# One-hot clusters kept twice, 32 rows apart, in a routed attention and bilinear FFN kernel

## The chip, the cores and the metric

The kernel runs on one core of a Trainium2 chip. A core has five engines that run side by side, each with its own instruction stream: TensorE (PE, with its weight loader PEld), VectorE (DVE), ScalarE (ACT), GpSimd (POOL) and SyncE (SP), which here only issues DMAs. The metric is the device time of one execution in microseconds (us), the median over several executions. The profile is of one execution; its "span" runs from the first to the last instruction.

## The reference

Attention in which a query sees only the keys of its own cluster, for 4 batches, 8 heads, 768 positions, head size 64, with 16 clusters; then a feed-forward block with a bilinear gate on 3072 tokens.

```python
q_assign = np.argmax(np.einsum('bhsd,hcd->bhsc', q_n, c_n), axis=-1)   # q_n, k_n, c_n: normalized
k_assign = np.argmax(np.einsum('bhsd,hcd->bhsc', k_n, c_n), axis=-1)
mask = q_assign[:, :, :, None] == k_assign[:, :, None, :]
scores = scale * np.matmul(q, k.transpose(0, 1, 3, 2))
scores = np.where(mask, scores, -1000000000.0)
...                                             # softmax over keys
attn_out = np.matmul(attn, v)
x = attn_out.transpose(0, 2, 1, 3).reshape(B * S, H * D)
return (x @ w_a) * (x @ w_b) @ w_out            # 512 -> 1536 -> 512
```

## The kernel before

**Pairs and groups.** Heads go two at a time: 16 pairs (4 batches of 4 pairs), `p` in the code. Head a = 0 lies on partitions 0 to 63, head a = 1 on 64 to 127. A pair's scores are made transposed, keys on the PSUM partitions: a unit `u` is one block of 128 keys (`j`, 0 to 5) against one half of the queries (`hf`, 384 of them), for both heads. Two units make a group, so a pair has 6 groups and the kernel 96. The main loop (L987) runs over groups `g`. In each, TensorE gets the scores of this group (`score`, L500), the product with v of the group before (`weigh`, L543), steps that prepare the next pair, and then pieces of the feed-forward block of an earlier batch, by a credit counter, until the next group.

**The mask as a matmul.** The cluster of every query and key is held as a one-hot vector of 16 rows per head, in bf16, in the tile `ohT`. For a key the row of its cluster holds 0 and the others a very large negative number; for a query the row of its cluster holds 1. The product of the two over those rows is 0 where the clusters agree and very negative where they don't. `score` writes it into PSUM first (L508, `start=True`), and the float32 product of q and k adds to it (L517, `stop=True`). ScalarE then takes the exponential (L524). A mask matmul multiplies over all 64 rows of its head, though only 16 carry clusters: the rest of the query rows hold zeros, left there by the first pairs, which write all 128 rows.

**Order inside `score`.** All four mask matmuls of a group stand first: unit 0 head 0, unit 0 head 1, unit 1 head 0, unit 1 head 1. Then the four score products in the same order, each of which the profile shows as two matmuls (float32 goes in two passes). Each of the four has its own PSUM bank. [...] In the profile the form "64*128" is a matmul over 64 rows with 128 output columns, "128*128" one over all rows, "128*64" and "128*32" ones with 64 and 32 output columns.

**How the one-hots come about.** For pairs 0 to 3 TensorE transposes them (`prep_onehot`, L394). For pairs 4 to 15 (`by_blocks`, L186, true from p = 4) VectorE transposes 32x32 blocks (`prep_by_blocks`, L411). That leaves four quarters `kq` of 384 positions each on partitions 32 kq: quarters 0 and 1 are the queries' halves, 2 and 3 the keys'. Within a quarter head a is on 16 rows. `one_hot_across` (L443) then moves each quarter of each head to its place in `ohTs[p]` with a small DMA on SP's queue: 4 quarters by 2 heads, 8 copies of 16 rows by 384 bf16, 12 KB each (L448). This is step 4 of the next pair's six, so it is issued during the fifth group of a pair, and the next pair's first group reads it. `ohTs` has two buffers.

**SP's queue.** One queue, in program order: the loads of q and k (L198), v (L235), weights (L263, two raw buffers), the one-hot copies (L448) and the output stores (L622). Each DMA signals on one of a few semaphores in turn.

Of the kernel before, what the change touches and what calls it, by code (L numbers as in the profile page):

```python
# [136 lines left out]
def short_path(nc, tc, ctx, c, cn, centroids_in, casts, n_far, q, k, v,  # L137
# [3 lines left out]
    B, H, S, D = q.shape  # L141
    NC = 16
# [6 lines left out]
    HB = S // 2  # L149
# [36 lines left out]
    def by_blocks(p):  # L186
        return p >= HP
# [141 lines left out]
    qkTs, ohTs, sims = {}, {}, {}  # L329
# [81 lines left out]
    def prep_by_blocks(p):  # L411

        qkTs[p] = qtp.tile([P, 2 * S], FP32, name="qkT")
        ohTs[p] = ohT_bufs[p % 2]
        NG = 24
        QT = slice(0, P // 2)
        KT = slice(P // 2, P)
        shape = (P, NG, NC)
        sim = simp.tile([P, NG, NC], FP32, name="sim")
        mx = small.tile([P, NG], FP32, name="mx")  # L420
        first = small.tile([P, NG], FP32, name="first")
        oh = oh_all[:, 0:3].rearrange("p n (g c) -> p (n g) c", c=NC)
        ohT = oh_all[:, 3:6].rearrange("p n e -> p (n e)")
        top = lambda t: t[:, :, None].broadcast_to(shape)
        v = nc.vector

        def across(w):
            v.transpose(out=qkTs[p][:, w * S:(w + 1) * S],
                        in_=qks[p][:, w].rearrange("p j d -> p (j d)"))

        def sims_across():
            v.transpose(out=sim.rearrange("p g c -> p (g c)"),
                        in_=sims[p][:, 0:HB])

        def one_hot():


            nc.gpsimd.tensor_tensor(out=oh[KT], in0=sim[KT], in1=top(first)[KT],
                                    op=ALU.subtract)
            v.tensor_tensor(out=oh[QT], in0=sim[QT], in1=top(first)[QT],  # L440
                            op=ALU.is_equal)

        def one_hot_across():  # L443
            v.transpose(out=ohT, in_=oh.rearrange("p g c -> p (g c)"))
            for a in range(2):
                for kq in range(4):
                    r = 32 * kq + a * NC
                    nc.sync.dma_start(  # L448
                        out=ohTs[p][a * D:a * D + NC, kq * HB:(kq + 1) * HB],
                        in_=ohT[r:r + NC, :])  # L450

        return [
            [lambda: across(0), lambda: across(1)],
            [sims_across],
            [lambda: v.tensor_reduce(out=mx, in_=sim, axis=AX.X, op=ALU.max),
             lambda: v.tensor_tensor(out=sim, in0=sim, in1=top(mx), op=ALU.is_ge),
             lambda: v.tensor_tensor(
                 out=sim, in0=sim, in1=rank_far[:, None, :].broadcast_to(shape),
                 op=ALU.mult),
             lambda: v.tensor_reduce(out=first, in_=sim, axis=AX.X, op=ALU.max)],  # L460
            [one_hot],
            [one_hot_across],
            [],
        ]
# [30 lines left out]
    def where(u):  # L495
        p, l = divmod(u, UPP)
        hf, j = divmod(l, NJ)
        return p, hf, j

    def score(us):  # L500
        tiles = []
        for u in us:
            p, hf, j = where(u)
            s = ps_s.tile([P, 2, 512], FP32, name="s")
            tiles.append(s)
            for a in range(2):
                r = slice(a * D, (a + 1) * D)
                nc.tensor.matmul(  # L508
                    out=s[:, a, 0:HB],
                    lhsT=ohTs[p][r, S + j * P:S + (j + 1) * P],  # L510
                    rhs=ohTs[p][r, hf * HB:(hf + 1) * HB],
                    start=True, stop=False)
        for u, s in zip(us, tiles):
            p, hf, j = where(u)
            for a in range(2):
                r = slice(a * D, (a + 1) * D)
                nc.tensor.matmul(  # L517
                    out=s[:, a, 0:HB],
                    lhsT=qkTs[p][r, S + j * P:S + (j + 1) * P],
                    rhs=qkTs[p][r, hf * HB:(hf + 1) * HB],  # L520
                    start=False, stop=True)
        for u, s in zip(us, tiles):
            pt = ptp.tile([P, 2, HB], FP32, name="pt")
            nc.scalar.activation(out=pt, in_=s[:, :, 0:HB], func=AF.Exp,  # L524
                                 scale=SCALE)
            probs[u] = pt
# [460 lines left out]
    for g in range(NG + 3):  # L987
        p, l = divmod(g, GPP)
# [4 lines left out]
        if g < NG:  # L993
            score(now)
# [300 lines left out]
```

## Time and profile before

| | us |
|---|---|
| median of 3 executions | 1072.19 (1072.11 to 1074.16) |
| the profiled execution | 1073.11, span 1071.4 |
| TensorE busy | 1046.6 |
| VectorE busy | 713.7 |
| GpSimd busy | 355.8 |
| ScalarE busy | 259.0 |

The granted TensorE clock is 0.995 of full. "Busy" is the union of an engine's instructions, and the end of a matmul is modelled by the profiler: two matmuls of one form overlap in the records, and a short gap between them need not show as idle. The starts are recorded, so the distance between two starts tells what the array really did. In the page's groups the score products (L517) hold 140.7 us of TensorE's busy time and those with v (L549) 145.1 us; the mask matmuls' group (L508) holds 48.2 us for 384 of them in 96 groups.

### The profile page before, as it was taken

Reading aid. Unit: us, or ns where it says so; the run is one execution under the profiler, and the core shown is the slowest. Engines: PE = TensorE matmul, PEld = TensorE weight load, DVE = VectorE, ACT = ScalarE, POOL = GpSimd, SP = SyncE. Lnnn points to the kernel's source line nnn. Section 1 sums busy time; section 2 is a strip of 40 time slices with the busy share of each in tenths; the row PEclk is TensorE's granted clock in tenths of the full one; section 3 lists DMA queues with packets and bytes.
Section 4 is the critical chain, followed back from the end, with each engine's and each line's share of the span. In section 5 each row is a group of like instructions: output and inputs, shape, how many; then the busy total and the mean of one; then the engine's idle time right before and its main releaser. Section 6 shows DMA issues by size and latency. Waiting matters only on the chain.

```text
span 1071.4 us, 13000 instructions
## 1 busy us (share of the span) xinstructions
PE 1046.6 (98%) x4719; PEld 602.5 (56%) x4719; DVE 713.7 (67%) x1396; ACT 259.0 (24%) x500; POOL 355.8 (33%) x329
## 2 busy tenths in 40 slices
PE   5999999999999999999999999999999999999997
PEld 3444455454556665454545766455455687555686
DVE  5888978787857537766666746667665745676762
ACT  4565423333322221122121221221212200000000
POOL 1221244454542323434444522344344410222200
PEclk8999999999999999999999999999999999999999
DMA  4335352525120120202030030300000000000001
GB/s 140 91 83 91 90 123 82 123 83 136 66 49 15 31 53 14 45 4 45 2 45 2 24 65 13 56 1 19 1 4 1 6 30 25 0 1 1 0 30 33
DMA packets 120504, 46.18 MB, mean 43 GB/s; under 512 B 106608, under 2 KB 115824, under 8 KB 120432
## 3 DMA queue, kind: packets, MB, share of 16 engines
q1 hardware_dynamic: 119456, 43.40, 17.9%
q10 hardware_dynamic: 976, 1.87, 0.5%
q8 instruction: 39, 0.64, 0.3%
q14 instruction: 33, 0.27, 0.1%
HBM read 37.78 MB, written 6.29 MB: 41 GB/s over the span
## 4 chain that ended last, share of the span: by engine, by line
PE 93%; DVE 5%; issue 0%; DMA 0%; POOL 0%; ACT 0%; DVEq 0%; POOLq 0%
PE m L732 30%; PE m L851 19%; PE O L549 12%; PE m L632 12%; PE s L517 11%; PE s L508 4%; PE m L572 3%; PE m L353 1%; DVE raw L693 1%; PE m L337 1%; DVE raw L715 1%; DVE xT L693 0%; DVE acc L538 0%; PE m L399 0%; DVE size L693 0%
## 5 line engine op out<-in xcount | busy, mean ns | idle before, releaser
L524 ACT ACTIVATE pt<-s 128x768 f32<-128x768 f32 x192 | 145.3, 809 | 313.7 <-PE s L517 258.5
L538 POOL TENSOR_TENSOR acc<-acc,pt 128x384 f32<-128x384 f32 x144 | 151.9, 1068 | 59.8 <-ACT pt L524 43.5
L747 POOL TENSOR_TENSOR h<-h,ha 128x384 f32<-128x384 f32 x72 | 72.6, 1016 | 235.8 <-DVE ha L742 234.3
L549 PE MATMUL O<-pt,v 128*64 128x384 f32 x768 | 145.1, 499 | 0.0
L517 PE MATMUL s<-qkT 64*128 64x384 f32 x768 | 140.7, 486 | 0.0
L742 DVE TENSOR_TENSOR ha<-ha,m 128x384 f32<-128x384 f32 x126 | 66.8, 546 | 74.1 <-PE m L732 73.3
L742 DVE TENSOR_TENSOR h<-h,m 128x384 f32<-128x384 f32 x126 | 67.4, 549 | 68.5 <-PE m L732 67.7
L538 DVE TENSOR_TENSOR acc<-acc,pt 128x384 f32<-128x384 f32 x96 | 72.8, 787 | 35.4 <-POOL acc L538 35.0
L549 PEld LDWEIGHTS O<-pt,v 128*64 128x64 f32 x768 | 46.6, 136 | 86.4 <-issue 82.1
L604 POOL TENSOR_TENSOR xT<-xT,acc 128x384 f32<-128x384 f32 x32 | 33.3, 1039 | 169.7 <-DVE acc L599 139.2
L517 PEld LDWEIGHTS s<-qkT 64*128 64x128 f32 x768 | 71.1, 188 | 32.0 <-issue 0.6
L851 PE MATMUL m<-wo_sb,h 128*128 128x256 f32 x384 | 87.5, 382 | 0.0
L851 PEld LDWEIGHTS m<-wo_sb,h 128*128 128x128 f32 x384 | 72.1, 190 | 16.0 <-issue 4.2
L732 PE MATMUL m<-raw 128*128 128x384 f32 x192 | 70.2, 488 | 0.9 <-DVE ha L742 0.9
L632 PE MATMUL m<-xT,wa_sb 128*128 128x384 f32 x192 | 67.1, 492 | 0.0
L632 PE MATMUL m<-xT,wb_sb 128*128 128x384 f32 x192 | 66.8, 491 | 0.0
L851 PE MATMUL m<-xT,h 128*128 128x256 f32 x288 | 65.4, 382 | 0.1
L851 PEld LDWEIGHTS m<-xT,h 128*128 128x128 f32 x288 | 54.1, 190 | 11.7 <-issue 1.7
L732 PE MATMUL m<-xT,wa_sb 128*128 128x384 f32 x144 | 53.0, 491 | 0.0
L732 PE MATMUL m<-xT,size 128*128 128x384 f32 x144 | 52.9, 490 | 0.0
L732 PE MATMUL m<-xT,wb_sb 128*128 128x384 f32 x144 | 52.9, 490 | 0.0
L632 PEld LDWEIGHTS m<-xT,wa_sb 128*128 128x128 f32 x192 | 35.5, 190 | 29.4 <-issue 3.6
(159 smaller groups left out, 1446.4 us busy)
## 6 DMA issues: line engine op xcount, KB each, us to landing
raw<-in_moe_w_out_dram SPq DMA_DIRECT2D x12, 512.0 KB, 3.4
raw<-in_moe_w_a_dram SPq DMA_DIRECT2D x11, 512.0 KB, 3.8
raw<-in_moe_w_b_dram SPq DMA_DIRECT2D x11, 512.0 KB, 3.6
qk<-in_q_dram SPq DMA_DIRECT2D x48, 96.0 KB, 3.1
qk<-in_k_dram SPq DMA_DIRECT2D x48, 96.0 KB, 3.6
v<-in_v_dram SPq DMA_DIRECT2D x24, 192.0 KB, 3.9
out_dram<-rest SPq DMA_DIRECT2D x24, 128.0 KB, 1.7
ohT<-oh SPq DMA_DIRECT2D x96, 12.0 KB, 1.8
```

The lines of the kernel that those rows point to most:

```text
L508: nc.tensor.matmul(out=s[:, a, 0:HB], lhsT=ohTs[p][r, S + j * P:S + (j + 1) * P], rhs=ohTs[p][r, hf * HB:(hf + 1) * HB], start=True, stop= ...
L517: nc.tensor.matmul(out=s[:, a, 0:HB], lhsT=qkTs[p][r, S + j * P:S + (j + 1) * P], rhs=qkTs[p][r, hf * HB:(hf + 1) * HB], start=False, stop ...
L524: nc.scalar.activation(out=pt, in_=s[:, :, 0:HB], func=AF.Exp, scale=SCALE)
L538: eng.tensor_tensor(out=acc[:, a, :], in0=probs[u - 1][:, a, :] if j == 1 else acc[:, a, :], in1=probs[u][:, a, :], op=ALU.add)
L549: nc.tensor.matmul(out=O_of[0][a * D:(a + 1) * D, 0:HB], lhsT=vs[p][:, a, j, :], rhs=probs[u][:, a, :], start=(j == 0), stop=(j == NJ - 1))
L572: nc.tensor.matmul(out=ps[a * D:(a + 1) * D, 0:HB], lhsT=ones, rhs=t[:, a, :], start=(n == 0), stop=(n == len(terms) - 1))
L604: nc.gpsimd.tensor_tensor(out=x, in0=x, in1=den, op=ALU.mult)
L632: nc.tensor.matmul(out=ps[:, 0:HB], lhsT=w_sb[:, ch, f * P:(f + 1) * P], rhs=xTs[b][:, ch, t0:t0 + HB], start=(ch == 0), stop=(ch == NCH - 1))
L732: nc.tensor.matmul(out=ps[:, 0:HB], lhsT=A[l][c], rhs=rhs[c], start=(c == 0), stop=(c == 1))
L742: nc.vector.tensor_tensor(out=out, in0=in0, in1=ps, op=op)
L747: nc.gpsimd.tensor_tensor(out=to, in0=to, in1=box[name], op=ALU.mult)
L851: nc.tensor.matmul(out=ps[:, 0:HN], lhsT=A[l][f // 3][:, f % 3, :], rhs=B[r][f // 2][:, f % 2, :], start=(f == 0), stop=(f == N2 - 1))
```

## The change

For pairs 4 to 15 every one-hot is kept twice: on rows 0 to 15 of its head's 64, as before, and again on rows 32 to 47. The mask matmuls of the second unit of a group read the second copy. Each mask matmul of these pairs now multiplies over 32 rows (16 of clusters and 16 that give zero) instead of 64, so the four of a group lie on rows 0 to 31, 64 to 95, 32 to 63 and 96 to 127. The number of DMAs of `one_hot_across` goes from 8 to 16 a pair, and their order changes: keys' first half, queries' first half, queries' second half, keys' second half, both heads and both copies of each before the next. The score products, and all of pairs 0 to 3, stay as they were. No instruction of VectorE, ScalarE or GpSimd changes.

```diff
         def one_hot_across():
             v.transpose(out=ohT, in_=oh.rearrange("p g c -> p (g c)"))
-            for a in range(2):
-                for kq in range(4):
+
+            for kq in (2, 0, 1, 3):
+                for a in range(2):
                     r = 32 * kq + a * NC
-                    nc.sync.dma_start(
-                        out=ohTs[p][a * D:a * D + NC, kq * HB:(kq + 1) * HB],
-                        in_=ohT[r:r + NC, :])
+                    for n in range(2):
+                        r0 = a * D + 32 * n
+                        nc.sync.dma_start(
+                            out=ohTs[p][r0:r0 + NC, kq * HB:(kq + 1) * HB],
+                            in_=ohT[r:r + NC, :])
...
     def score(us):
         tiles = []
-        for u in us:
+        for n, u in enumerate(us):
             p, hf, j = where(u)
             s = ps_s.tile([P, 2, 512], FP32, name="s")
             tiles.append(s)
             for a in range(2):
                 r = slice(a * D, (a + 1) * D)
+                if by_blocks(p):
+                    r = slice(a * D + 32 * n, a * D + 32 * n + 32)
                 nc.tensor.matmul(
                     out=s[:, a, 0:HB],
```

## The prediction

> **What bounds the kernel now.** I read the page first: the share of busy time, then the chain that ended last, by engine.
>
> ```profile
> PE 1046.6 (98%) x4719; PEld 602.5 (56%) x4719; DVE 713.7 (67%) x1396; ACT 259.0 (24%) x500; POOL 355.8 (33%) x329
> ...
> PE 93%; DVE 5%; issue 0%; DMA 0%; POOL 0%; ACT 0%; DVEq 0%; POOLq 0%
> ```
>
> TensorE is busy all the time and the chain runs through it, so a nanosecond saved or added in TensorE's stream is one in the span. The list of TensorE's waits on other engines holds under 19 us, most of it in the first 20 us. What the page hides is that "busy" includes the gaps between matmuls, since their ends are modelled. So I read the mask matmuls' own line next.
>
> ```profile
> L508 PEld LDWEIGHTS <-ohT x384: 92/95/110, 17.1 to 853.7; 64*128 64x128 bf16 x192
> L508 PE MATMUL s<-ohT x384: 322/332/524, 17.4 to 853.9; 64*128 64x384 bf16 x192
> ...
>   issue: 43.3, 90
> ```
>
> Before 90 of the 96 mask groups the weight loader stands idle for nothing that the profile can name, 0.48 us each. To see why, I took the timeline in narrow windows around one group of pair 12, first the matmuls into and through the group (columns: start, us from start to last end, engine, line, operation; the last number counts matmuls).
>
> ```profile
> 606.92 0.59 PE L851 MATMUL m<-wo_sb,h 128*128 128x256 f32 x2
> ...
> 607.35 0.38 PE L851 MATMUL m<-wo_sb,h 128*128 128x256 f32 x1
> 607.66 0.50 PE L508 MATMUL s<-ohT 64*128 64x384 bf16 x4
> 607.84 0.33 PE L508 MATMUL s<-ohT 64*128 64x384 bf16 x2
> 608.00 0.48 PE L517 MATMUL s<-qkT 64*128 64x384 f32 x1
> 608.97 0.49 PE L517 MATMUL s<-qkT 64*128 64x384 f32 x2
> 609.38 0.54 PE L549 MATMUL O<-pt,v 128*64 128x384 f32 x2
> 609.75 0.49 PE L549 MATMUL O<-pt,v 128*64 128x384 f32 x2
> ```
>
> Starts, not durations, are to be read. Two L851 matmuls of one kind start 0.22 apart (606.92 to 607.35 is two steps), which is their streaming time. From the last of them (128 rows, 128 columns of the array) to the first mask matmul (64 rows) it is 0.31: 0.09 more. The masks run two at a time, second pair 0.17 to 0.18 after the first, and the score products follow 0.16 later: no extra, because both are "64*128". Score pairs follow each other by 0.32 (two passes of 384 float32 columns). From the last to L549, of form "128*64", it is 0.41: again 0.09 more. The loads and the way out of two more forms:
>
> ```profile
> 607.84 0.19 PEld L517 LDWEIGHTS s<-qkT 64*128 64x128 f32 x1
> 610.82 0.30 PEld L851 LDWEIGHTS m<-wo_sb,h 128*128 128x128 f32 x2 [0.60 <-issue]
> 611.14 0.19 PEld L851 LDWEIGHTS m<-wo_sb,h 128*128 128x128 f32 x1
> 622.32 0.49 PE L353 MATMUL m<-qkT,cTb 128*32 128x384 f32 x1
> 622.74 0.54 PE L572 MATMUL m<-acc,ones 128*64 128x384 f32 x2
> ```
>
> The score weights are loaded while the second mask pair runs (607.84), so nothing shows. After a change of form they aren't: L851's first load stands at 610.82 beside its first matmul, the next matmul comes at 611.14, 0.32 later where 0.22 is its rate. Even 128*32 to 128*64, one column tiling to another, costs 0.42 for a 0.32 stream. Every change of form in this trace costs **0.09 to 0.10 us of emptying, and then the first weight load in the open**: 0.10 for 128 float32 columns (L851), 0.05 for 64 (L549: 0.37 against 0.32), 0.01 for 128 bf16 columns (the mask pair's 0.17 against 0.16).
>
> [...] The trace shows two row groups at once (mask pairs) and four column groups (L353), no four row groups. [...]
>
> **The change, part by part.** It touches pairs 4 to 15, 12 pairs of 6 groups: 72 groups; the other 24 keep 64-row masks.
>
> 1. Four masks at once. Before: 607.66 to 608.00, 0.335 us from first mask to first score (0.173 + 0.162 by the medians of the starts). After: four starts 3 ns apart (0.01), the first load 0.01, one stream 0.16, so 0.18 if nothing else came: 0.154 saved.
> 2. A new change of form, 32-row masks to 64-row scores. The way into the masks is a change already, and the way out of the scores too; this one is added. [...] Bounds: nothing, or what the five kinds of change seen cost, 0.09 to 0.10. I take 0.095, as none was free, columns to columns included.
> 3. The score weights' load comes into the open: 128 float32 columns, 0.10 (L851; 0.104 in the unrounded starts). Bounds 0 (loaded while the masks run, as now) and 0.10; I take 0.10, as no load went ahead of a change of form.
>
> Sum per group: −0.154 + 0.095 + 0.104 = +0.045 us; 72 groups: **+3.2 us**. It lies on TensorE, with nothing beside it to hide it.
>
> 4. Eight copies a pair more on SP's queue. Now eight take 5 us to issue; the page gives 1.8 us to landing.
>
> ```profile
> 293.74 4.93 SPq L448 DMA_DIRECT2D ohT<-oh  x8
> 311.37 2.14 SPq L198 DMA_DIRECT2D qk<-in_q_dram  x4
> ...
> 301.21 0.34 PE L508 MATMUL s<-ohT 64*128 64x384 bf16 x2
> ```
>
> This is pair 7, the tightest of the twelve: first copy 7.5 us ahead of its first mask. Copies go 0.63 apart. The new order (key and query quarters 2, 0 first) puts all that the first group needs into the first eight: landed at 293.74 + 7 x 0.63 + 1.8 = 299.95, before 301.21. The last lands at 305.0; the second group's masks stand at 312.3 and need it first. So nothing waits. Moved past 5 us more of issue: in pair 7 the loads of q and k at 311.4, which finds the queue free at 303.8; in pair 4 a weight load issued at 124.27 that follows the copies (117.97 to 123.0): about 129.3, landing 3.7 later at 133.0, where VectorE's rounding began at 131.28. That is 1.7 us of VectorE once, bounded between 0 (three PSUM buffers of 1.29 us of matmuls each cover it) and 1.7; I take 0. Output stores in pairs 9 to 14 come up to 5 us later; their buffers are written again several us on (the `rest` tile stored at 603.87 is next written at 613.99). I take 0, up to 1 in the range.
> 5. First groups wait on twice as many copies: in the built program 24 mask instructions carry two semaphores instead of 12; the extra wait is 51 ns in the trace. 12 x 0.051 = 0.6 us at most; it lies in the emptying before the masks (pair 7's first group: 0.42 after a 0.32 stream, as elsewhere), so 0.
>
> VectorE, ScalarE and GpSimd execute the same instructions in the same order. Against the profiled span of 1071.4 the sum gives 1074.6. The timed median is 1072.19, so 1075.4; I forecast **1075.5 us**, with a hair for 4 and 5.
>
> **Rivals.**
> - *The row tilings need no emptying* (faster). Both are row tilings with full columns, and the array's row groups may be independent enough that 64-row work follows 32-row work as masks follow masks. Then part 1 alone: 72 x 0.154 = −11.1, 1061.1 us. For it: no change between row tilings is in the trace. Against: column to column costs full price.
> - *It empties, but the weights are loaded meanwhile.* Without part 3: 72 x (−0.154 + 0.095) = −4.2, 1068.0 us. Against: at every change seen the loader's first load starts with the first matmul.
> - *The four don't run at once* (slower still): four outputs into four PSUM banks, where two are shown. The second pair then costs 0.16 more: 3.2 + 11.5 = +14.7, 1087 us. [...]
> - *SP's queue decides*: if a first group had to wait for all sixteen copies, landing 11.3 us after the first issue, pairs whose first copy leads by less (7.5 us in pair 7, 9.1 to 10.6 in five others) would stop TensorE, 10.9 us in all, by the sum of what their leads lack: with the 3.2 above 1086 us. The decisive point is a lead under 11.3. Against: the built program's first group waits on eight.
>
> **How the numbers follow.** Forecast case 0.68, with its own range 1073.5 to 1078.5 (0.02 to 0.065 a group, and up to 1.5 for parts 4 and 5). No emptying 0.16; weights loaded meanwhile 0.08; not at once 0.05; SP's queue 0.03. For 8 in 10 the range takes in the forecast and the loads-meanwhile case, 0.76, and the slower edge: 1067.0 to 1078.5. No change that a measurement can tell is within 0.2%, 2.1 us. Of the forecast case 0.09 falls there (under 0.03 a group). Slower: 0.68 − 0.09 + 0.08 = 0.67; faster: 0.16 + 0.08 = 0.24.
>
> **What would show it.** In the after-trace's narrow timeline: four mask starts within 0.01 (part 1); first mask to first score 0.28 (0.18 means no emptying, 0.34 or more not at once); first to second score pair 0.42 instead of 0.32 (part 3), its load at the first score's start. Mask and score lines then have more idle "issue" time ahead of the score loads. SP: sixteen issues over 10 us, and no DMA among TensorE's waits. The forecast is wrong if the first gap is 0.18, or if TensorE waits for copies or for VectorE in pairs 4 to 15.

## The result, and the profile after

| | before | changed |
|---|---|---|
| median, us | 1072.99 (6 executions) | 1077.24 (6 executions) |
| ratio | 1 | 1.0041 (95% interval 1.0028 to 1.0054) |
| span of the profiled execution, us | 1071.4 | 1075.0 |

The changed kernel is slower by 0.41%, some 4.4 us (3.0 to 5.8). The forecast was 1075.5 us, slower by 3.3. The time lies inside the stated range, on the long side of the centre. One execution of the kernel before, of the 23 in the third comparison below, took 1217.82 us at a granted clock of 0.85 and is left out of all ratios and counts.

The page first: TensorE's busy time, the chain by engine, and the groups of the score products and of their weight loads.

```profile
PE 1050.6 (98%) x4719; PEld 598.1 (56%) x4719; DVE 714.1 (66%) x1396; ACT 259.4 (24%) x500; POOL 355.5 (33%) x329
...
PE 93%; DVE 5%; issue 0%; DMA 0%; POOL 0%; ACT 0%; DVEq 0%; POOLq 0%
...
L522 PE MATMUL s<-qkT 64*128 64x384 f32 x768 | 149.5, 509 | 0.0
...
L522 PEld LDWEIGHTS s<-qkT 64*128 64x128 f32 x768 | 68.2, 189 | 39.9 <-issue 14.0
```

Of the engines only TensorE grew: 4.0 us more busy, with VectorE, ScalarE and GpSimd within half a microsecond of before and the weight loader 4.4 us less busy. The chain runs through the same engines in the same shares. The score products (L517 before, L522 now) went from 140.7 to 149.5 us although they didn't change, and their weight loads now stand idle for 14.0 us without a releaser, where before it was 0.6. That fits an array that empties between masks and scores. "Emptying" names the extra time between two starts at a change of form, 0.09 to 0.10 us; the starts below show the time, not what the array does in it.

The timeline in narrow windows around the same group of pair 12 (start, us to the last end, engine, line, form, count) answers the one shown before:

```profile
610.00 0.38 PE L856 MATMUL m<-wo_sb,h 128*128 128x256 f32 x1
610.31 0.34 PE L513 MATMUL s<-ohT 32*128 32x384 bf16 x4
610.31 0.10 PEld L513 LDWEIGHTS <-ohT 32*128 32x128 bf16 x4 [0.33 <-issue]
610.59 0.59 PE L522 MATMUL s<-qkT 64*128 64x384 f32 x2
610.58 0.30 PEld L522 LDWEIGHTS s<-qkT 64*128 64x128 f32 x4 [0.17 <-issue]
611.01 0.49 PE L522 MATMUL s<-qkT 64*128 64x384 f32 x2
```

A score pair here is two matmul records side by side: one of the two float32 passes, for both heads of a unit. All four masks run together: four matmuls cover 0.34 us where two pairs covered 0.50. The first score comes 0.28 after the first mask (0.34 before), but its weight load stands beside it (610.58) instead of under the masks, and the second score pair comes 0.42 later, not 0.32. By the medians of the unrounded starts over the 72 groups, first mask to first score went from 0.335 to 0.271, first to second score pair from 0.323 to 0.427, and first mask to last score from 1.306 to 1.350. That is **0.043 to 0.044 us a group, 3.1 us in 72 groups**. The first 24 groups are the same in both traces. From there on the changed kernel's trace falls behind before's by 0.043 us with every group, except at groups 53 and 54 (near 410 us), where it loses 1.5 us more at once; that loss is taken up below.

### The profile page after: what moved, and what is told of

The parts are those of the page before. It is cut to its first block, busy times and chain, and to the rows that moved or that the text cites. A ratio compares the mean times of both kernels' runs of the same rounds, so it can differ in the third digit from the quotient of the medians.

```text
span 1075.0 us, 13105 instructions
## 1 busy us (share of the span) xinstructions
PE 1050.6 (98%) x4719; PEld 598.1 (56%) x4719; DVE 714.1 (66%) x1396; ACT 259.4 (24%) x500; POOL 355.5 (33%) x329
## 4 chain that ended last, share of the span: by engine, by line
PE 93%; DVE 5%; issue 0%; DMA 0%; POOL 0%; ACT 0%; DVEq 0%; POOLq 0%
PE m L737 30%; PE m L856 19%; PE s L522 12%; PE O L554 12%; PE m L637 12%; PE m L577 3%; PE s L513 3%; PE m L353 1%; DVE raw L698 1%; PE m L337 1%; DVE raw L720 1%; DVE xT L698 0%; DVE acc L543 0%; DVE size L698 0%; DVE ha L747 0%
## 5 line engine op out<-in xcount | busy, mean ns | idle before, releaser
L522 PE MATMUL s<-qkT 64*128 64x384 f32 x768 | 149.5, 509 | 0.0
L522 PEld LDWEIGHTS s<-qkT 64*128 64x128 f32 x768 | 68.2, 189 | 39.9 <-issue 14.0
```

The costliest lines, as they stand in the source:

```text
L522: nc.tensor.matmul(out=s[:, a, 0:HB], lhsT=qkTs[p][r, S + j * P:S + (j + 1) * P], rhs=qkTs[p][r, hf * HB:(hf + 1) * HB], start=False, stop ...
```

## The experiments

**The changed kernel again, and its copies alone.** The first is the changed kernel itself. The second keeps its sixteen copies and takes back the rows:

```diff
-                if by_blocks(p):
-                    r = slice(a * D + 32 * n, a * D + 32 * n + 32)
```

> The changed kernel again, beside the kernel with its copies alone. Theory F (the added change of form from 32-row masks to 64-row scores costs its emptying and an open weight load, 0.043 us in each of 72 groups by the starts in its trace): 3.1 us slower than before. Rival Q (the eight copies more per pair on SP's queue, and what they push back, add about 1.2 us to that): 4.3 us slower.

> Sixteen copies in the new order, but the masks over 64 rows as before (both copies are then summed, which leaves the mask's sense: 0 or very negative). Theory F: no difference from before (within 0.5 us), first mask to second score pair 0.66 us in every group. Rival Q: 1 to 1.5 us slower than before, seen as TensorE or VectorE waiting in pairs 4 to 15.

Measured: the copies alone 1073.75 us against 1073.46 for before, ratio 1.0001 (0.9993 to 1.0010), every group's first mask to second score pair 0.658 us. From group 20 on its trace keeps its distance to before's within 0.02 us. So copies, queue and semaphores cost nothing that shows, and theory F holds there. The changed kernel itself came to 1078.96, ratio 1.0050 (1.0037 to 1.0064): some 5.4 us, above F's 3.1 and above Q's 4.3. Q falls with the copies; F is left with some 2 us (1 to 4 by the interval) that it doesn't explain.

**Two masks at a time over 32 rows.** On the kernel before:

```diff
-                r = slice(a * D, (a + 1) * D)
+                r = slice(a * D, a * D + 32 if by_blocks(p) else (a + 1) * D)
```

> Masks of pairs 4 to 15 over 32 rows, but both units of a group read the first copy, so two run at a time; eight copies as before. Theory F: first mask to first score 0.434 us (0.173 + 0.003 + 0.160 + 0.095 and 0.003), first to second score pair 0.427, so 0.203 a group over before: 14.6 us slower than before, 11.5 slower than the changed kernel, which is what four at once is worth. Rival W (a stream of 32-row masks is slow in itself and there is no emptying): first mask to first score under 0.36 us, and the second score pair at 0.32.

Measured: 1089.62 us, ratio 1.0149 (1.0133 to 1.0164), so 16.0 us slower than before and 10.7 over the changed kernel, where F said 14.6 and 11.5. Its timeline, near 630 us:

```profile
629.76 0.50 PE L508 MATMUL s<-ohT 32*128 32x384 bf16 x4
629.93 0.33 PE L508 MATMUL s<-ohT 32*128 32x384 bf16 x2
630.19 0.59 PE L517 MATMUL s<-qkT 64*128 64x384 f32 x2
```

Here both pairs lie on the same rows, and the second comes 0.17 after the first (in the changed kernel, on rows of its own, 7 ns after it). So masks go together where their rows differ. The first score comes 0.43 after the first mask, and the second score pair 0.427 after that (unrounded medians). So the 32-row stream itself is as long as the 64-row one, the emptying is there, and W falls. First mask to second score pair is 0.854 (0.658 before): 0.196 a group, 14.1 us; the trace also has two drops of the clock, of which more below. Against the changed kernel's 0.698, four at once is worth 0.156 us a group.

**What meets the change first.** Only the first unit's masks go over 32 rows; the second unit's stay at 64.

```diff
+                if by_blocks(p) and n == 0:
+                    r = slice(a * D, a * D + 32)
```

> First unit's masks over 32 rows, second unit's over 64 as before, then the scores; eight copies as before. The change of form now meets a bf16 mask pair first, and the scores' float32 weights can load during it. Theory F (what stands open after a change is the first load of whatever comes next): first mask to second mask pair 0.271 us, from there to the first score 0.162 to 0.173, first to second score pair 0.323, in all 0.767 against 0.658: 7.8 us slower than before. Rival L (after a change of row tiling the scores' float32 load always stands open, or the load's 0.104 belongs to the change itself): 0.10 more, second mask pair to first score 0.27 or second score pair at 0.42: 15 us slower.

```profile
624.27 0.34 PE L510 MATMUL s<-ohT 32*128 32x384 bf16 x2
624.53 0.34 PE L510 MATMUL s<-ohT 64*128 64x384 bf16 x2
624.54 0.20 PEld L519 LDWEIGHTS s<-qkT 64*128 64x128 f32 x2
624.71 0.81 PE L519 MATMUL s<-qkT 64*128 64x384 f32 x4
```

From 32-row to 64-row masks it is 0.267, from there to the first score 0.172, and from the first to the second score pair 0.323 (unrounded medians): 0.762 in all, where F said 0.767. The float32 weights are loaded under the second mask pair again (624.54), and the 0.104 is gone: L falls. So the open load isn't a property of the change of form; it is the first load of whatever follows. Timed, 1082.55 us, ratio 1.0083 (1.0068 to 1.0099): 9 us slower where the starts give 7.5; its trace holds one drop of the clock, too.

**More changes.** The changed kernel with each unit's two score products directly behind its two masks, inside the loop over units:

```diff
-        for u, s in zip(us, tiles):
-            p, hf, j = where(u)
...
+            masks()
+            products()
```

> The changed kernel with each unit's scores directly behind its masks: in pairs 4 to 15 the array goes 32, 64, 32, 64 rows instead of 32, 64. Two more changes of form and an extra mask stream. Theory F: each change costs 0.095 and the open load behind it (0.104 scores, 0.013 masks), so from the end of the first unit's scores to the second's first is 0.095 + 0.013 + 0.163 + 0.095 more, and 0.104 for the load: 0.47 us a group over the changed kernel, 34 us in all. Rival B (going back from 64 to 32 rows, half the array or less, is free): 0.37 a group, 27 us.

```profile
630.74 0.33 PE L515 MATMUL s<-ohT 32*128 32x384 bf16 x2
631.00 0.92 PE L524 MATMUL s<-qkT 64*128 64x384 f32 x4
631.85 0.33 PE L515 MATMUL s<-ohT 32*128 32x384 bf16 x2
632.11 0.92 PE L524 MATMUL s<-qkT 64*128 64x384 f32 x4
632.96 0.54 PE L559 MATMUL O<-pt,v 128*64 128x384 f32 x2
```

From 64 back to 32 rows it is 0.42 after the last score pair for a stream of 0.32, so 0.10 again: B falls. First mask to the products with v is 2.22 here, against 1.76 in the changed kernel (medians of the starts): 0.46 a group where F said 0.47. The time, 1108.26 us, ratio to before 1.0320 (1.0304 to 1.0335), is 29.5 over the changed kernel's 1078.76 beside it, where F said 34 and the starts give 33. Part of the difference is in the idle gaps told of next: 1.70 us each in this trace, 2.15 in the changed kernel's, and no execution with a mean clock under 0.995; the rest isn't explained.

**The rest over 3.1 us.** The traces gave a second suspect. The clock in windows of two traces, before and changed, around 410 us (columns: window, its length, busy us of PE, PEld, DVE, ACT and POOL with their counts, PEclk, DMA share, GB/s):

```profile
408.00:412.00 4.00, 1.80 (x6) 0.80 (x5) 3.85 (x13) 0.48 (x1) 0.00 (x0) 1.00 0.02 6
412.00:416.00 4.00, 4.00 (x23) 1.63 (x22) 1.02 (x2) 1.51 (x2) 0.00 (x0) 1.00 0.09 23
```

```profile
408.00:412.00 4.00, 1.85 (x7) 0.84 (x6) 3.93 (x14) 0.48 (x1) 0.00 (x0) 1.00 0.02 6
412.00:416.00 4.00, 4.00 (x15) 1.43 (x13) 1.18 (x3) 0.72 (x1) 0.00 (x0) 0.57 0.08 20
```

In both, TensorE idles for 2.2 us near 409, where VectorE's combinations for the next batch's up products are late. The first four matmuls after that gap, before and changed:

```profile
410.94 1.56 PE L732 MATMUL m<-raw,comb 128*128 128x384 f32 x4 [2.20 <-DVE comb L715]
```

```profile
411.20 1.96 PE L737 MATMUL m<-raw,comb 128*128 128x384 f32 x4 [2.15 <-DVE comb L720]
```

In the changed kernel's trace the granted clock then falls to half, from 412.22 to 415.63, 3.413 us: 4 us at 0.57 are 1.7 us lost. That is where, group by group, the trace lost its 1.5 us. The stretches of one clock begin whole multiples of 3.413 us apart in the records of the clock: in the changed kernel's trace 2, 1, 115, 1 and 192 of them, in before's 1, 2 and 307. I call 3.413 us between two such marks a window, and continued the windows from the first mark through each trace. What the clock goes by isn't shown, only what followed what. In the changed kernel's trace the gap, 409.05 to 411.20, lies in the window from 408.80 to 412.22, and the half clock begins where that window ends. In before's an edge at 409.62 cuts it, 0.88 us in one window and 1.31 in the next, and the clock stays full. I did this for the gaps of 2.0 us and more (two to a trace, near 409 and 667) in the traces of before, changed, its two repeats, copies alone, two by two and one pair: each of the six gaps that lay wholly inside a window was followed by the drop, none of the eight that crossed an edge. A closer measure is TensorE's idle time within one window. In all twelve traces, those of the experiments below included, every window between 100 and 1000 us with 1.99 us of it or more (eight) was followed by the drop (2.15 in the changed kernel's), and none with 1.95 us or less (at most 1.32 in before's). Two experiments fill the gaps, with the change and without, and the changed kernel runs beside them:

```diff
+            if first:
+                return half_1, half_2, [p1, p2, p6, p7, p4, p5, p3]
             return half_1, half_2, [p1, p6, p2, p7, p4, p5, p3]
```

`p1` then also copies its product to where `p6` adds its own.

> The changed kernel, but in the first part of each batch's up products the product that needs no combination on VectorE (12 by 21) stands second instead of third, so that 1.29 us of matmuls lie in each of the two idle gaps of 2.2 us (near 409 and 667 us). Theory D (the traces show the TensorE clock at half for 3.4 us after a gap that lies within one window of 3.413 us, and that is what the change's time has over 3.1 us): 2.6 us less from the two gaps, no half clock in mid-run, so 1.5 to 2.5 us more off the changed kernel where it shows such drops; 3.1 us over the unchanged kernel with the same filling. Rival S (the rest over 3.1 us is in the start or in the copies): still 4.5 to 5.5 us over that kernel.

> The kernel before with the same filling of the two gaps, and without the change. Theory D: 2.6 us faster than before, up to 3.2 where before shows drops of the clock; that would be faster than both kernels. Rival V (VectorE stays the bound of that stretch and the products only move the wait): no gain.

> The changed kernel beside the others of this call. Theory F with D: 3.1 us slower than before, and up to 2.5 more in the executions in which the clock falls in mid-run; median 1.5 to 2.5 above what the two traces' starts explain. Rival S: every execution 4.3 to 5.5 us slower than before.

| kernel | median, us | ratio to before (95%) | executions with mean clock of 0.994 or less |
|---|---|---|---|
| before | 1073.78 | 1 | 3 of 22 |
| before, gaps filled | 1071.62 | 0.9978 (0.9968 to 0.9987) | 0 of 10 |
| changed, gaps filled | 1074.64 | 1.0001 (0.9993 to 1.0009) | 0 of 14 |
| changed | 1078.76 | 1.0045 (1.0032 to 1.0057) | 5 of 6 |

The last column is a lower bound. A mean clock also holds the half clock at the kernel's start (3.4 us in some traces, 6.8 in others) and at its end, and two traces of the changed kernel that hold a drop have means of 0.995 and 0.996. None of the six traces without a drop has a mean under 0.995.

With the gaps filled, the change costs 3.0 us by the medians (2.5 by the ratios), which is what the starts say, and S falls. (The changed kernel alone, with its six executions 4.5 to 5.6 us over before, would fit S as well as D; the filled pair decides.) Without the change, filling the gaps is faster than both kernels by more than its interval, so V, no gain, falls. The gain, 2.2 us by the medians, is less than D's 2.6, as the gaps shrank less than expected. The same place in before with gaps filled, to be read beside the 2.20 us above:

```profile
411.11 1.56 PE L733 MATMUL m<-xT,wa_sb 128*128 128x384 f32 x4 [1.27 <-DVE rest L866]
```

The product that was moved up waits itself now, for VectorE's addition of an earlier down product (L866). So 0.93 us were won a gap, not 1.29. That VectorE frees a PSUM buffer there, behind its combinations, is my reading of the line; it wasn't tested. In the traces of the filled kernels gaps of 1.2 to 1.3 us brought no drop, two of them inside a window for their whole length.

**Why the changed kernel meets the drop more often.** The change moves the first gap by 29 groups of 0.043, 1.25 us. The last two experiments move it in the kernel before, with matmuls in group 30 whose result nobody reads, in the second kernel six instead of two, over 384 columns five times and 112 once:

```diff
+        if g == 30:
+            ps = ps_m.tile([P, 512], FP32, name="m")
+            for n in (384, 384):
+                nc.tensor.matmul(out=ps[:, 0:n], lhsT=wa_sb[:, 0, 0:P],
+                                 rhs=xTs[0][:, 0, 0:n], start=True, stop=True)
```

> The kernel before with two matmuls more in group 30, whose result nobody reads: four streams of 0.322 us, so 1.29 us more of TensorE, put well ahead of the first idle gap (near 409 us). The change brings 29 x 0.043 = 1.25 us by that gap. Theory P (the clock's windows stand about the same to the kernel's start in most executions, so that what decides a drop is where the gap lies; 1.25 us later it lies inside a window): mean clock of 0.994 or less in most executions, and 2.9 us slower or more, 1.3 of them the matmuls. Rival U (the windows lie anywhere; the drops are as rare as in before, and the changed kernel's were chance): 1.3 us slower, clock 0.995 or more in nearly all.

> The same with six matmuls of that kind, the last over 112 columns: 5 x 0.645 + 0.19 = 3.41 us, one whole window. Theory P: the gap lies to the windows as in before, drops as rare as there, so 3.4 us slower and no more, clock 0.995 or more in nearly all executions. Rival U: the same 3.4. A rival in which the extra work itself brings the drops: clock 0.994 or less here too, 5 us slower.

Measured against 1074.04 for before: 1.29 later 1076.05, ratio 1.0024 (1.0013 to 1.0034), 2 of 8 executions at a clock of 0.992 and the others at 0.996 or more; 3.41 later 1077.36, ratio 1.0031 (1.0019 to 1.0043), none of 6. The second costs about what its matmuls take, 3.3 us of 3.4. The first costs 2.0 us by the medians and 2.6 by the ratio, between U's 1.3 and P's 2.9. By the mean clocks P asked for most executions and got a quarter. But that is a lower bound, and a mean of 0.996 doesn't rule a drop out, so the clocks decide for neither.

The traces say more. In that of the first kernel both gaps are followed by a drop, the first gap wholly in a window, the second reaching 0.07 us past its edge, with 2.14 us inside; in that of the second kernel neither is. The windows do not stand the same to the kernel's start, as P put it, but they do to the stream of matmuls. TensorE's idle gap near 110 us, ahead of all that these kernels change, begins 0.02 to 0.25 of a window after an edge in all twelve traces. The gap near 409 begins 0.55 to 0.74 into a window in before, in copies alone and in the second kernel, and crosses the window's end. With the change, or with the 1.29 us of matmuls, it begins 0.02 to 0.13 into one and lies inside. So in the traced executions the shift decides, as P says. How many of the others had a drop stays open: the changed kernel had 12 of 17 executions at 0.994 or less in all comparisons, and before 4 of 53 in the three that list its clocks, both counts being lower bounds.

## Why the prediction was right

**The bound.** TensorE's stream, as read. Extra time appears there alone, and the change's own part of the result is a sum of starts. The 2.2 us gaps that bring the drops of the clock were in the list of TensorE's waits; they were rightly read as small, but what a gap can do to the clock was no part of the prediction.

**Part 1, four at once.** Right. Four starts lie within 0.010 us, as taken. The trace before showed row groups two at a time, 3 ns apart, so four at once was an estimate from those. Worth 0.156 a group (0.854 − 0.698 between the two-by-two experiment and the changed kernel), for 0.154 predicted.

**Part 2, the added change of form.** Right in kind, a little too dear in size: 0.276 was its sum from first mask to first score (0.28 as written) and 0.271 was measured, so by that sum the emptying is 0.09 and not 0.095. (The prediction calls the 0.32 between score pairs two float32 passes; it is one pass of two heads side by side, and the sum doesn't hang on it.) The two directions cost about the same: from 32 to 64 rows the second mask pair comes 0.267 after the first (one pair) where it was 0.173 without a change, and from 64 back to 32 rows the start comes 0.42 after a stream of 0.32 (by unit). The rival without emptying, which would have made the change worth 11 us, is out.

**Part 3, the open load.** Right: 0.427 for the second score pair, 0.104 over its stream, as forecast from the 128-column load elsewhere. The rival with the weights loaded meanwhile is out with it. The experiment with one pair shows that it goes away (0.323) when a short-loading bf16 pair comes first.

**Parts 4 and 5, copies and semaphores.** Right. Sixteen copies take twice the time to issue and no matmul waits for them, in pair 7 too:

```profile
293.39 9.99 SPq L451 DMA_DIRECT2D ohT<-oh  x16
...
301.05 0.34 PE L513 MATMUL s<-ohT 32*128 32x384 bf16 x4
```

The late weight load of pair 4 did come, VectorE waiting 0.97 us for it at 131.43 where up to 1.7 was allowed, and no matmul followed it late: the next groups keep their distance to those of before, but for the 0.043 us of each.

```profile
131.43 0.43 DVE L277 TENSOR_SCALAR wa_sb<-raw 128x512 int32<-128x512 int32 x1 [0.97 <-DMA raw<-in_moe_w_a_dram]
```

**The sum.** +3.2 predicted for TensorE, +3.1 in the starts, +2.5 to +3.0 timed once the gaps are filled. What the prediction lacked is a term: the result is 4.4 us in the first comparison and 4.8 and 5.4 in the two later ones, and the 1.3 to 2.3 above 3.1 come with the drops of the clock. That they do is shown by the filled gaps, and in the trace by the 1.5 us lost at once; that the change's shift of the gap brings them is shown for the traced executions alone. That the range held the result is in part luck: it allowed up to 0.065 us a group and 1.5 us for parts 4 and 5, which cost nothing, and the clock took up that room.

**Not tried.** If the scores too ran over 32 rows, each head's 64 in two halves, no change of form would be needed between masks and scores. But the two halves of a score would have to add up in the same place of PSUM. Whether they can run at once then, and at what cost, isn't shown: no run here has it.

## What to carry to other kernels

Count the changes of array form in a stream before tiling matmuls more finely: here each cost 0.09 to 0.10 us and then the first weight load in the open, so packing that by the estimate saved 0.154 us a group lost 0.043 in all, as it added one change and exposed a 128-column float32 load of 0.104. Read it from the starts of matmuls, since busy shares and durations hide it. If a change can't be avoided, a matmul with a short weight load behind it can hide the long load that follows: here a bf16 pair took the 0.104 us away, though that kernel was slower in all, as its masks no longer ran four at once. An idle gap of TensorE can cost more than its length: here 2 us of idle time within one window (1.99 or more in eight of them) were followed by 3.4 us at half speed.

## What was not expected of the hardware

Gaps of 2.0 to 2.2 us were followed by 3.413 us at half the clock when they lay inside one window, at a price of 1.5 us by the groups' starts (1.7 by 4 us at a mean clock of 0.57). Gaps of 1.2 to 1.3 us inside one didn't, nor did one of 1.7 us in the by-unit trace. What sorts all twelve traces is the idle time within one window: a drop after 1.99 us and more, none after 1.95 and less. No run lies between, and only one comes close from below, the second gap of copies alone with 1.95. Where a gap stood to the windows followed from the stream ahead of it: the change's 1.25 us moved the first gap from across an edge to inside a window in every traced execution.
